# Units 0 and 1 without the first merge, their row steps shared by VectorE and GpSimd; the last row steps of units 2 and 3 on VectorE

## The chip, the cores and the metric

The kernel runs on one core of a Trainium2 chip. The metric is the device time of one execution in microseconds; 2084.89 us is the median of three runs of the kernel before. The engines are named TensorE (PE in the rows, its weight loads PEld), VectorE (DVE), ScalarE (ACT), GpSimd (POOL) and SyncE (SP, which issues most DMAs). Each engine works through a queue of its own, and the queues meet at semaphores.

## The reference, cut to what matters

A delta-rule attention over 768 positions, 4 x 8 heads of size 48, feeds a mixture of 8 experts (all of them computed, mixed by a normalised table P), and then a layer with h cos(h):

```python
def _attn_ref(q, k, v, beta):
    k_n = k / (np.linalg.norm(k, axis=-1, keepdims=True) + 1e-06)
    for t in range(S):
        y[:, :, t] = np.einsum('bhd,bhde->bhe', q[:, :, t], state)
        v_old = np.einsum('bhde,bhd->bhe', state, kt)
        state = state + bt[:, :, :, None] * np.einsum('bhd,bhe->bhde', kt, vt - v_old)
def _moe_ref(x, w_gate, w1, w2):
    ...
    for e in range(E):
        out += P[:, e:e + 1] * (np.maximum(x @ w1[e], 0.0) @ w2[e])
def _moe2_ref(x, w_in, w_out):
    h = x @ w_in
    return (h * np.cos(h)) @ w_out
```

## The kernel before, in words

**Units.** The 768 positions are cut into 12 units of 64 (`C`). Inside a unit the 64 sequential updates of the reference become a triangular system per head: I plus a strictly lower triangular matrix N of beta times the products of keys. Its inverse is made for blocks of 32 (`CB`), for two units at once: 2 units x 16 head pairs (`NS` = 16, four partition groups of 32) lie on the partitions after a 32 x 32 transpose, so that one instruction treats all systems of both units, and a 32 x 32 system lies along the free dimension (`Nsys`, `Xsys`, or `ns0` for units 0 and 1).

**Row steps.** `inv_ops` (line 372) returns a list of 32 closures: the transpose of `Nst` into `Nsys` (VectorE, L374), a select that starts `Xsys` (GpSimd, L377), and the row steps j = 1 to 30. Step j multiplies column j of N, below row j, with row j of the result so far (L388) and adds that to all rows below (L392): two instructions of (31 - j) x j elements per partition, on the engine `eng`, which is GpSimd for all steps. Row j + 1 of the result is complete after step j. The closures are queued in `inv_q`, and `inv_some(n)` takes n of them off and issues them.

**Units 0 and 1** come first. `inv16` (line 399) does row steps on VectorE for both 16 x 16 diagonal blocks at once (14 steps, two instructions each, L408 and L409). The rest is added on TensorE: `merge16_a` multiplies the lower left block of N (`n0`, masked with `m16`), `merge16_y` (VectorE) scales with beta, `merge16_b` multiplies with the first block's inverse, and `merge16_c` adds the result to `tx` and transposes it into `dm`. `tx` and `dm` hold the inverse in its two orientations.

**From the inverse on.** For unit u: `pe_Z1` and `pe_Z2` (TensorE, evictions by ScalarE into `W` and by VectorE into `Bs`) extend the inverse from 32 to 64, `pe_KS` subtracts what the state already gives (`D`), `pe_U` multiplies with the inverse and VectorE writes `U` (L532), `pe_S` adds to the state `S`, `pe_PU` and `pe_QS` make the output rows `Y`, and `pe_XT` transposes them into `xb`, the expert layer's input. The first expert matmul (`H`, L139) needs `xb` of units 0 and 1. In the dense part `half()` issues expert matmuls in between (`moe0_h`, `moe0_y`, evicted by `relu_split`, L156 and L157).

**What sets the order.** Everything is issued under a manual schedule: each engine's queue holds its instructions in the order in which the Python code calls them. The prologue (from `warm(48, p23)` on) is written out by hand; behind it, `tick(u, seq)` walks through the strings in `SEQ`, a letter per step ("U" is `pe_U`, "r" empties `inv_q` and makes `dm`, "R" makes `tx`, "i" starts the next system, "m" is an expert half step, a digit picks the unit). `beta_raw`, `go_beta`, `raw`, `norm_*` and `n_dve` in the prologue scale with beta and the norms; `pp_mask` and `pp_ev` apply the causal mask to the query products `Pp`.

Of the kernel before, what the change touches and what calls it, by code (L numbers as in the profile page):

```python
# [38 lines left out]
def kernel(  # L39
# [331 lines left out]

    def inv_ops(nst, nsys, xsys, tmp, eng):

        ops = [lambda: nc.vector.transpose(out=nsys, in_=nst.rearrange("p s t -> p t s"))]  # L374
# [21 lines left out]
        return ops


    def inv16(xsys, tmp):
        def blk(t0, i0, dt, di, n, j):  # L400
            a = xsys[:, t0:t0 + 1, i0:i0 + 1]
            return bass.AP(a.tensor, a.offset, [a.ap[0], [16 * CB + 16, 2], [dt, n], [di, j]])

        def step(j):
            n = 15 - j
            a = tmp[:, 0:2 * n * j].rearrange("p (a t i) -> p a t i", a=2, t=n)
            x = blk(j + 1, 0, CB, 1, n, j)
            nc.vector.tensor_tensor(out=a, in0=blk(j + 1, j, CB, 0, n, j), in1=blk(j, 0, 0, 1, n, j), op=ALU.mult)  # L408
            nc.vector.tensor_tensor(out=x, in0=x, in1=a, op=ALU.add)  # L409

        return [lambda j=j: step(j) for j in range(1, 15)]

    def merge16_a(u, n, bank, y=True):
# [8 lines left out]
        if y:
            merge16_y(u, bank)

    def merge16_y(u, bank):
        ym[u] = ap2.tile([128, NS, CB], F32, tag="W", name="ym")
        nc.vector.tensor_tensor(
            out=ym[u][:, :, 0:16], in0=bank[:, 0:NS * 16].rearrange("p (s t) -> p s t", t=16),
            in1=betam[:, u, :, None].to_broadcast([128, NS, 16]), op=ALU.mult,
        )  # L430

    def merge16_b(u, bank, s0=0, s1=NS):
        y = ym[u]
        for s in range(s0, s1):
            for p in range(4):
                r = slice(p * CB, p * CB + CB)
                nc.tensor.matmul(
                    out=bank[r, (NS + s) * 16:(NS + s + 1) * 16], lhsT=dm[r, u * NS + s, :], rhs=y[r, s, 0:16],
                    start=True, stop=True, skip_group_check=True,
                )  # L440
# [257 lines left out]
    with tc.manual_schedule():  # L698
# [171 lines left out]
        for u in range(2):  # L870
            nc.scalar.activation(
                out=betam[:, u].rearrange("p (i m) -> p i m", i=2),
                in_=beta_sb[:, u, 0:NS].rearrange("p (m i) -> p i m", i=2), func=ACTF.Copy, scale=hm[:, 4:5],
            )
# [29 lines left out]
        merge16_b(0, pab[:, 0])
        merge16_b(1, pab[:, 1])
        inv_q.extend(inv_ops(Nst, Nsys, Xsys, tmp, nc.gpsimd))
        inv_some(1)
        merge16_c(0, pab[:, 0])
        bs_act(0)
        inv_some(99)  # L910
        pe_Z1(0, pab[:, 0])
# [1 line left out]
        pe_Z1(1, pab[:, 1])
        pp_ev(1, xs0.rearrange("p a c -> p (a c)").rearrange("p (s c) -> p s c", c=C), p01)
        pe_KS(0)
        nc.vector.transpose(out=beta_x, in_=bw[1].rearrange("p (u t) -> p u t", t=CB))
        pe_Z2(0, p01[:, 0])
        beta_raw_x(0)
# [1012 lines left out]
```

## Time and profile before

| | us |
|---|---|
| median of 3 runs (2082.3 to 2086.13) | 2084.89 |
| the profiled execution, its time | 2088.02 |
| the profiled execution, its span | 2085.9 |
| TensorE busy | 2053.4 |
| VectorE busy | 1461.4 |
| GpSimd busy | 905.7 |
| ScalarE busy | 866.1 |

All rows below come from one profiled execution, in microseconds from the start of its span. A busy share is an average over the whole span; which engine ends last in a stretch is read from the windows and the waits of that stretch.

### The profile page before, as it was taken

The numbers are of one execution on the slowest core, as the hardware profiler recorded it, in microseconds if no ns is written. First come the engines' busy times: TensorE is split into PE (matmuls) and PEld (weight loads), VectorE is DVE, ScalarE is ACT, GpSimd is POOL, SyncE is SP. The second block draws the span as 40 slices with busy tenths as digits, with TensorE's granted clock in tenths as the row PEclk, the third lists the DMA queues.
The fourth block names the chain that finished last, engine by engine and source line by source line (L and its number), as shares of the span: only waits on it lengthen the run. The fifth ranks groups of instructions, "written<-read, shape, count | busy, mean of one in ns | idle before, by whom it ended". The sixth has DMA issues, their size and how long they took to land.

```text
span 2085.9 us, 39694 instructions
## 1 busy us (share of the span) xinstructions
PE 2053.4 (98%) x16132; PEld 1729.9 (83%) x16132; DVE 1461.4 (70%) x2253; ACT 866.1 (42%) x1436; POOL 905.7 (43%) x1012
## 2 busy tenths in 40 slices
PE   7999999999999999999999999999999999999999
PEld 6887888778888888888888888888888889999998
DVE  6665537677677777777767787787788666666665
ACT  3442333344444444434333333333333356666664
POOL 4676660156555655544353333333333343333331
PEclk7899999999999999999999999999999999999999
DMA  5532346765554544453684544535354551011000
GB/s 94 127 94 57 78 127 196 296 237 164 193 172 157 204 169 169 177 179 136 249 302 143 173 151 142 173 120 192 130 174 144 185 201 31 1 31 31 16 16 15
DMA packets 212470, 294.39 MB, mean 141 GB/s; under 512 B 86160, under 2 KB 159344, under 8 KB 212288
## 3 DMA queue, kind: packets, MB, share of 16 engines
q1 hardware_dynamic: 208368, 284.20, 41.3%
q0 software_dynamic: 1664, 6.49, 0.9%
q8 instruction: 126, 2.06, 0.4%
q10 hardware_dynamic: 2256, 1.18, 0.2%
q14 instruction: 56, 0.46, 0.1%
HBM read 188.95 MB, written 113.87 MB: 145 GB/s over the span
## 4 chain that ended last, share of the span: by engine, by line
PE 91%; POOL 3%; DVE 2%; SPq 1%; issue 1%; DMA 1%; ACT 1%; ACTq 0%; POOLq 0%; DVEq 0%
PE ps L150 36%; PE ps L1469 27%; PE ps L1759 10%; PE ps L1717 9%; PE ps L139 4%; PE ps L313 1%; POOL w1t L392 1%; POOL w1t L388 1%; PE ps L498 1%; PE ps L281 1%; PE ps L526 1%; PE ps L463 0%; PE ps L556 0%; PE ps L475 0%; PE ps L573 0%
## 5 line engine op out<-in xcount | busy, mean ns | idle before, releaser
L150 PE MATMUL ps<-mh,w2t 128*128 128x512 f32 x3060 | 749.3, 389 | 0.4 <-DVE cth L1505 0.4
L150 PEld LDWEIGHTS ps<-mh,w2t 128*128 128x128 f32 x3060 | 573.5, 188 | 122.0 <-DVE cth L1505 3.3
L1469 PE MATMUL ps<-T,w1t 128*128 128x512 f32 x2520 | 627.2, 389 | 1.9 <-ACT ct L1474 0.8
L1506 POOL TENSOR_TENSOR accp<-accp,cth 128x512 f32<-128x512 f32 x246 | 320.3, 1333 | 562.8 <-DVE cth L1505 562.8
L1469 PEld LDWEIGHTS ps<-T,w1t 128*128 128x128 f32 x2520 | 472.2, 188 | 101.6 <-ACT ct L1474 1.3
L156 ACT ACTIVATE mh<-ps 128x512 fp32r<-128x512 f32 x340 | 203.6, 600 | 620.7 <-PE ps L1469 237.3
L157 DVE SCALAR_TENSOR_TENSOR mh<-ps,mh 128x512 fp32r<-128x512 f32 x340 | 228.8, 688 | 176.8 <-ACT mh L156 175.4
L1474 ACT ACTIVATE scr<-ps 128x512 f32<-128x512 f32 x224 | 134.5, 600 | 163.7 <-PE ps L1469 154.4
L1726 POOL TENSOR_SCALAR tp<-tp 128x512 f32<-128x512 f32 x92 | 91.5, 994 | 204.2 <-ACT tp L1725 204.2
L1505 DVE TENSOR_TENSOR cth<-ps,scr 128x512 f32<-128x512 f32 x246 | 154.3, 684 | 15.2 <-PE ps L150 13.3
L1740 DVE TENSOR_TENSOR tp<-tp,ps 128x512 f32<-128x512 f32 x96 | 66.1, 688 | 133.5 <-ACT tp L1739 133.5
L1477 DVE TENSOR_TENSOR ps<-scr,ps 128x512 f32<-128x512 f32 x168 | 116.5, 694 | 54.6 <-PE ps L1469 53.1
L139 PE MATMUL ps<-xb,w1t 128*128 128x512 f32 (+1 forms) x441 | 111.4, 397 | 0.0
L150 PE MATMUL ps<-h,w2t 128*128 128x512 f32 x396 | 100.8, 400 | 0.0
L1477 DVE TENSOR_TENSOR scr<-ps,scr 128x512 f32<-128x512 f32 x112 | 77.1, 689 | 30.5 <-PE ps L1469 29.2
L139 PEld LDWEIGHTS ps<-xb,w1t 128*128 128x128 f32 x441 | 78.6, 188 | 17.1 <-DVE xb L579 0.9
L1309 DVE TENSOR_TENSOR w1t<-wraw,w1t 128x512 fp32r<-128x512 f32 (+2 forms) x81 | 74.7, 934 | 19.1 <-ACT w1t L1306 17.9
L150 PEld LDWEIGHTS ps<-h,w2t 128*128 128x128 f32 x396 | 73.4, 190 | 15.7 <-issue 0.2
L392 POOL TENSOR_TENSOR w1t<-w1t 128x30 f32<-128x30 f32 (+9 forms) x150 | 80.7, 538 | 11.7
L1717 PE MATMUL ps<-xx,cw 128*128 128x512 f32 x360 | 84.0, 390 | 0.0
L388 POOL TENSOR_TENSOR w1t<-Nsys,w1t 128x30 f32<-128x30 f32 (+9 forms) x150 | 77.9, 520 | 11.4
L1725 ACT ACTIVATE tp<-ps 128x512 f32<-128x512 f32 x96 | 56.2, 586 | 63.5 <-PE ps L1717 63.5
(286 smaller groups left out, 2769.2 us busy)
## 6 DMA issues: line engine op xcount, KB each, us to landing
wss<-w1t SPq DMA_DIRECT2D x56, 768.0 KB
w1t<-wss SPq DMA_DIRECT2D x56, 768.0 KB
w2t<-w2c SPq DMA_DIRECT2D x56, 384.0 KB
T<-tsc SPq DMA_DIRECT2D x22, 512.0 KB
scr<-pts SPq DMA_DIRECT2D x44, 256.0 KB
w2c<-in_moe_w_dram SPq DMA_DIRECT2D x28, 384.0 KB
wss<-w1t SPq DMA_DIRECT2D x28, 384.0 KB
w1t<-wss SPq DMA_DIRECT2D x28, 384.0 KB
```

The source lines that it names most:

```text
L139: nc.tensor.matmul(out=ps[:, :nn], lhsT=w[:, a, kk, fs], rhs=x[:, b, kk, c0:c0 + nn], start=(i == 0), stop=(i == 3 * KD - 1),)
L150: nc.tensor.matmul(out=banks[kd], lhsT=w[:, a, f % 2, kd * 128:(kd + 1) * 128], rhs=h[:, b, :], start=(first and b == 0 and a == 0), stop= ...
L156: nc.scalar.activation(out=h[:, 0, :nn], in_=ps[:, :nn], func=ACTF.Relu)
L157: nc.vector.scalar_tensor_tensor(out=h[:, 1, :nn], in0=ps[:, :nn], scalar=0.0, in1=h[:, 0, :nn].bitcast(F32), op0=ALU.max, op1=ALU.subtract,)
L392: eng.tensor_tensor(out=xsys[:, j + 1:, 0:j], in0=xsys[:, j + 1:, 0:j], in1=a, op=ALU.add)
L1469: nc.tensor.matmul(out=bank, lhsT=s_of(n, nm, a), rhs=T[:, b, :], start=start and q == 0, stop=q == 2, skip_group_check=True)
L1474: nc.scalar.activation(out=out, in_=in_, func=ACTF.Copy, scale=scale)
L1477: nc.vector.tensor_tensor(out=out, in0=a, in1=b, op=op)
L1505: nc.vector.tensor_tensor(out=c, in0=yb[kd], in1=pslot[t], op=ALU.mult)
L1506: nc.gpsimd.tensor_tensor(out=a[:, kd, :], in0=a[:, kd, :], in1=c, op=ALU.add)
L1717: nc.tensor.matmul(out=hb2(i), lhsT=net_w1(f, a, kk), rhs=x2[b](c, kk), start=(j == 0), stop=(j == 3 * KD - 1))
L1759: nc.tensor.matmul(out=ybk[t][:, :DM], lhsT=h[:, a, ts], rhs=net_w2(f, c), start=(f == 0 and j == 0), stop=(f == FT2 - 1 and j == 2),)
```

## The change

For units 0 and 1 the first merge goes (`merge16_a`, `merge16_y`, `betam`). `inv16` now runs row steps over all 32 rows for the first 16 columns on VectorE, and the second diagonal block on GpSimd beside it; step 15 is split by rows between the two. The mask `hm[:, 4]` is inverted and applied by ScalarE to a copy of the half-made inverse that takes the place of N in `n0`, and the merge that is left (`merge16_b`) multiplies that with the second block's inverse. Scaling of `Go` for units 0 and 1 and the mask of unit 1 go to GpSimd. `Go` of units 2 and 3 is copied by ScalarE (`raw`) and scaled later on VectorE. Z1, Z2 and U of unit 0, its state and the second beta transpose move into the prologue, in part ahead of the system of units 2 and 3. Of that system's 32 closures the prologue issues all but the last 8, which stand in `inv_last` until the letter "r" of the next tick; `inv_ops` gets `last=22`, from which step on VectorE is used. The later systems stay on GpSimd.

```diff
-SEQ = ("U0 a0 y1 o2 S0 x1 b0 P0 K1 o3 k1 v U1 X0 P1 S1 X1 H0 x2",
+SEQ = ("P0 y1 a0 x1 K1 b0 o2 k1 o3 v U1 X0 P1 S1 X1 H0 x2",
...
-    def inv_ops(nst, nsys, xsys, tmp, eng):
+    def inv_ops(nst, nsys, xsys, tmp, eng, last=CB):
...
         def mul(j):
             n = CB - 1 - j
+            e = nc.vector if j >= last else eng
...
+        def step(eng, t0, i0, j, a, r0=0, r1=CB):
+            r0 = max(r0, t0 + j + 1)
+            n = r1 - r0
+            a = a[:, 0:n * j].rearrange("p (t i) -> p t i", t=n)
+            x = xsys[:, r0:r1, i0:i0 + j]
+            eng.tensor_tensor(
+                out=a, in0=xsys[:, r0:r1, i0 + j:i0 + j + 1].to_broadcast([128, n, j]),
+                in1=xsys[:, t0 + j:t0 + j + 1, i0:i0 + j].to_broadcast([128, n, j]), op=ALU.mult,
+            )
+            eng.tensor_tensor(out=x, in0=x, in1=a, op=ALU.add)
+
+        for j in range(1, 16):
+            step(nc.vector, 0, 0, j, tmp[:, 0:256], 0, CB if j < 15 else 24)
+        for j in range(1, 15):
+            step(nc.gpsimd, 16, 16, j, tmp[:, 256:512])
+        step(nc.gpsimd, 0, 0, 15, tmp[:, 256:512], 24)
...
     def merge16_c(u, bank):
         x = tx[:, u * NS:(u + 1) * NS, 16:32]
-        nc.vector.tensor_tensor(
-            out=x, in0=x, in1=bank[:, NS * 16:2 * NS * 16].rearrange("p (s t) -> p s t", t=16), op=ALU.add
+        nc.vector.scalar_tensor_tensor(
+            out=x, in0=x, scalar=hm[:, 4:5], in1=bank[:, 0:NS * 16].rearrange("p (s t) -> p s t", t=16),
+            op0=ALU.mult, op1=ALU.add,
         )
...
+    def inv16_dm(xsys, n):
+        nc.vector.transpose(
+            out=dm.rearrange("p s j -> p j s")[:, 0:16], in_=xsys.rearrange("p t j -> p j t")[:, 0:16]
+        )
+        for u in range(2):
+            s = slice(u * NS, (u + 1) * NS)
+            nc.scalar.activation(out=n[:, s, 0:16], in_=dm[:, s, 0:16], func=ACTF.Copy, scale=hm[:, 4:5])
...
+        pp_raw(1, xs0.rearrange("p a c -> p (a c)").rearrange("p (s c) -> p s c", c=C), p01)
+        nc.gpsimd.memset(n0[:, :, 16:CB], 0.0)
+        inv16(ns0, W0.rearrange("p s t -> p (s t)"))
+        go_beta(0, nc.gpsimd)
+        go_beta(1, nc.gpsimd)
         v_scale(0, nc.gpsimd)
         pp_mask(0)
-        for x in inv16(ns0, W0.rearrange("p s t -> p (s t)")):
-            x()
-        inv_tx(ns0)
-        inv_dm(ns0)
+        pp_mask(1)
+        inv16_dm(ns0, n0)
+        inv16_tx(ns0, 16)
+        inv16_tx(ns0, 0)
+        merge16_b(0, n0, pab[:, 0])
         norm_red(2)
         norm_red(3)
         norm_a(2, 4)
+        merge16_c(0, pab[:, 0])
+        bs_act(0, 0)
+        merge16_b(1, n0, pab[:, 1])
         norm_b(2, 4)
         norm_sqr(2)
...
+        pe_Z1(0, p01[:, 0])
+        bs_act(0, 1)
         norm_pe(2, pab[:, 0])
+        nc.vector.transpose(out=beta_x, in_=bw[1].rearrange("p (u t) -> p u t", t=CB))
+        beta_raw_x(0)
         beta_raw(2, pab[:, 0])
         n_dve(2, pcd)
         n_dve(3, p23)
...
+        pe_KS(0)
+        pe_Z2(0, p01[:, 1])
         merge16_c(1, pab[:, 1])
...
+        inv_q.extend(inv_ops(Nst, Nsys, Xsys, tmp, nc.gpsimd, 22))
+        inv_some(len(inv_q) - 8)
+        inv_last.extend(inv_q)
+        inv_q.clear()
+        pe_U(0)
+        load_v(2)
+        pe_Z1(1, p01[:, 0])
+        pe_S(0)
+        load_k(5)
...
                 elif c == "r" and u + 1 < NU:
                     inv_some(99)
+                    while inv_last:
+                        inv_last.pop(0)()
                     inv_dm(Xsys)
```

VectorE's queue in the prologue, from the system of units 2 and 3 (`Nsys`) to U of unit 0, before (the bracket names what an instruction waits for):

```order
L374 STREAM_TRANSPOSE Nsys<-w2t 128x1024 [waits Pool_49]
L444 TENSOR_TENSOR tx<-tx,ps_154 128x16x16 [waits PE_49]
L447 STREAM_TRANSPOSE dm<-tx 128x512 [waits DVE_49]
L444 TENSOR_TENSOR tx<-tx,ps_154 128x16x16 [waits PE_49]
L447 STREAM_TRANSPOSE dm<-tx 128x512 [waits DVE_49]
L818 TENSOR_TENSOR scr_192<-ps_154,mask 128x1024
...
L481 SCALAR_TENSOR_TENSOR Bs<-ps_154,hm,Bs 128x16x32 [waits PE_49,Activation_49]
L799 TENSOR_TENSOR beta_x<-beta_x,nrm 128x2x16 [waits DVE_49]
L532 TENSOR_TENSOR U<-ps_154,beta_x 128x2x8x48 [waits DVE_49,PE_49,Activation_49]
```

and after the change, from the two N evictions (`w2t`) on, where `w1t` is the tile that `Xsys` and the scratch of the row steps lie in:

```order
L806 SCALAR_TENSOR_TENSOR w2t<-ps_154,hm,w2t 128x512 x2
L478 SCALAR_TENSOR_TENSOR Bs<-ps_154,hm,Bs 128x16x32 [waits PE_49,Activation_49]
L430 SCALAR_TENSOR_TENSOR tx<-tx,hm,ps_154 128x16x16
L434 STREAM_TRANSPOSE dm<-tx 128x512 [waits DVE_49]
L374 STREAM_TRANSPOSE Nsys<-w2t 128x1024 [waits Pool_49]
L389 TENSOR_TENSOR w1t<-Nsys,w1t 128x198 [waits DVE_49,Pool_49]
L393 TENSOR_TENSOR w1t<-w1t 128x9x22 [waits DVE_49]
L529 TENSOR_TENSOR U<-ps_154,beta_x 128x2x8x48 [waits PE_49]
L543 TENSOR_TENSOR S_185<-S_184,ps_154 128x2x2x192 [waits PE_49]
```

The transpose into `Nsys` has moved behind Bs of unit 0 and the merge of unit 1, and row step 22 (198 elements, then 9 rows of 22) has come between it and U of unit 0.

GpSimd's queue behind the set-up (`ones` is its last instruction), before:

```order
L754 MEMSET ones 128x128
L239 TENSOR_TENSOR v<-v,dv 128x768
L829 TENSOR_TENSOR Pp<-Pp,mask 128x1024
L345 TENSOR_TENSOR w2t<-w2t,beta_sb 128x512 x2
L377 AFFINE_SELECT w1t<-Nsys 128x1024
```

and after, with the row steps of the second block of units 0 and 1 (`scr_192` holds `ns0` and, from `xs0` on, Pp of unit 1, `W_193` the scratch):

```order
L751 MEMSET ones 128x128
L882 MEMSET scr_192 128x32x16
L407 TENSOR_TENSOR W_193<-scr_192 128x14
...
L407 TENSOR_TENSOR W_193<-scr_192 128x120
L411 TENSOR_TENSOR scr_192<-scr_192,W_193 128x8x15
L770 TENSOR_TENSOR Go<-Go,beta_sb 128x512 x2
L239 TENSOR_TENSOR v<-v,dv 128x768
L828 TENSOR_TENSOR Pp<-Pp,mask 128x1024
L828 TENSOR_TENSOR scr_192<-scr_192,mask 128x1024
L345 TENSOR_TENSOR w2t<-w2t,beta_sb 128x512 x2
L377 AFFINE_SELECT w1t<-Nsys 128x1024
```

Thirty row-step instructions, two scalings of Go and a second mask now stand ahead of the beta scaling (L345) of the system of units 2 and 3.

VectorE's queue in the tick that follows, around `dm` of units 2 and 3, before:

```order
L265 TENSOR_TENSOR kr_190<-kr_190,nrm 128x16x48
L157 SCALAR_TENSOR_TENSOR h<-ps_154,h 128x512
L452 STREAM_TRANSPOSE dm<-w1t 128x32x32
L235 TENSOR_REDUCE nrm<-sq 128x16
L248 TENSOR_SCALAR nrm<-nrm 128x16
```

and after:

```order
L265 TENSOR_TENSOR kr_190<-kr_190,nrm 128x16x48
L157 SCALAR_TENSOR_TENSOR h<-ps_154,h 128x512
L389 TENSOR_TENSOR w1t<-Nsys,w1t 128x184
L393 TENSOR_TENSOR w1t<-w1t 128x8x23
L389 TENSOR_TENSOR w1t<-Nsys,w1t 128x168
...
L393 TENSOR_TENSOR w1t<-w1t 128x30
L448 STREAM_TRANSPOSE dm<-w1t 128x32x32
L235 TENSOR_REDUCE nrm<-sq 128x16
```

Steps 23 to 30, sixteen instructions, now stand between h and `dm`.

## Rows read from the trace of the kernel before

**Rows 1.** The page's first part: busy us (share of the span) xinstructions of TensorE.

```profile
PE 2053.4 (98%) x16132; PEld 1729.9 (83%) x16132; DVE 1461.4 (70%) x2253; ACT 866.1 (42%) x1436; POOL 905.7 (43%) x1012
```

**Rows 2.** Windows: length, busy us (x instructions) of PE, PEld, DVE, ACT, POOL, PEclk, DMA.

```profile
25.00:50.00 25.00, 17.66 (x761) 16.29 (x761) 19.11 (x39) 5.51 (x9) 9.49 (x14) 0.50 0.43 91
50.00:75.00 25.00, 21.01 (x675) 19.84 (x676) 12.49 (x16) 6.19 (x10) 22.26 (x36) 0.58 0.54 125
75.00:100.00 25.00, 24.94 (x366) 20.40 (x365) 20.62 (x31) 12.60 (x20) 13.57 (x20) 1.00 0.49 117
```

**Rows 3.** TensorE's waits from 420 us on: total us, times, longest; the first.

```profile
PE ps L1469 <- ACT ct L1474: 0.8, 1, 0.8
```

**Rows 4.** Timeline of PE: start us, us, line, out<-in, xcount [idle before <-releaser].

```profile
43.21 1.90 PE L437 MATMUL ps<-ym,dm 32*32 32x16 f32 x128 [0.55 <-issue]
...
74.48 2.75 PE L139 MATMUL ps<-xb,w1t 128*128 128x256 f32 x18
...
95.56 1.20 PE L463 MATMUL ps<-dm,Go 32*32 32x32 f32 x64
...
97.90 1.06 PE L281 MATMUL ps<-ident,kr 128*128 128x128 f32 x8
```

**Rows 5.** Timeline of DVE, 20 to 57 us, the start's chain.

```profile
24.16 0.27 DVE L408 TENSOR_TENSOR W<-scr 128x112 f32<-128x112 f32 x1
...
27.81 0.19 DVE L409 TENSOR_TENSOR scr<-scr,W 128x28 f32<-128x28 f32 x1
28.03 1.94 DVE L455 STREAM_TRANSPOSE tx<-scr 128x1024 f32<-128x1024 f32 x1
...
31.64 1.78 DVE L235 TENSOR_REDUCE nrm<-sq 128x16 f32<-128x768 f32 x2
...
33.98 0.18 DVE L256 TENSOR_SCALAR nrm<-nrm 128x32 f32<-128x32 f32 x1 [0.30 <-ACT nrm L255]
...
35.65 0.19 DVE L779 TENSOR_TENSOR nrm<-nrm 128x32 f32<-128x32 f32 x1
...
40.85 1.40 DVE L807 SCALAR_TENSOR_TENSOR w2t<-ps,hm,w2t 128x512 f32<-128x512 f32 x2
43.77 1.92 DVE L374 STREAM_TRANSPOSE Nsys<-w2t 128x1024 f32<-128x1024 f32 x1 [1.53 <-POOL w2t L345]
...
46.03 0.71 DVE L447 STREAM_TRANSPOSE dm<-tx 128x512 f32<-128x512 f32 x1
...
56.20 0.96 DVE L532 TENSOR_TENSOR U<-ps,beta_x 128x768 f32<-128x768 f32 x1 [2.30 <-PE ps L526]
```

**Rows 6.** Timeline of POOL, 45 to 76 us: select and row steps of units 2, 3.

```profile
45.76 1.27 POOL L377 TENSOR_SCALAR_AFFINE_SELECT w1t<-Nsys 128x1024 f32<-128x1024 f32 x1 [2.02 <-DVE Nsys L374]
...
47.17 0.25 POOL L388 TENSOR_TENSOR w1t<-Nsys,w1t 128x30 f32<-128x30 f32 x1
47.50 0.26 POOL L392 TENSOR_TENSOR w1t<-w1t 128x30 f32<-128x30 f32 x1
...
57.66 1.18 POOL L388 TENSOR_TENSOR w1t<-Nsys,w1t 128x220 f32<-128x220 f32 x1
...
62.34 1.24 POOL L392 TENSOR_TENSOR w1t<-w1t 128x234 f32<-128x234 f32 x1
...
74.20 0.61 POOL L392 TENSOR_TENSOR w1t<-w1t 128x210 f32<-128x210 f32 x1
```

**Rows 7.** Timeline of DVE, 88 to 120 us, the first tick and beyond.

```profile
89.81 0.68 DVE L157 SCALAR_TENSOR_TENSOR h<-ps,h 128x512 fp32r<-128x512 f32 x1
90.41 2.07 DVE L452 STREAM_TRANSPOSE dm<-w1t 128x1024 f32<-128x1024 f32 x1
...
95.21 2.46 DVE L265 TENSOR_TENSOR kr<-kr,nrm 128x768 f32<-128x768 f32 x1
...
119.25 0.46 DVE L256 TENSOR_SCALAR nrm<-nrm 128x16 f32<-128x16 f32 x1
```

**Rows 8.** Timeline of POOL at 95 us, a weight split.

```profile
95.05 1.82 POOL L129 TENSOR_TENSOR w1t<-stg,w1t 128x768 fp32r<-128x768 f32 x1 [9.48 <-ACT w1t L128]
```

More of the change, by code (lines that the diff above doesn't have):

```diff
@@ L177 @@
     beta_sb = ap1.tile([128, NU, CB], F32, name="beta_sb")
-    betam = ap1.tile([128, 2, NS], F32, name="betam")
+    ap1.tile([128, 2, NS], F32, name="pad2")
     beta_x = ap1.tile([128, NU, CB], F32, name="beta_x")
@@ L391, in mul @@
             )
-            eng.tensor_tensor(out=xsys[:, j + 1:, 0:j], in0=xsys[:, j + 1:, 0:j], in1=a, op=ALU.add)
+            e.tensor_tensor(out=xsys[:, j + 1:, 0:j], in0=xsys[:, j + 1:, 0:j], in1=a, op=ALU.add)
         for j in range(1, CB - 1):
@@ L399, in inv16, with merge16_b @@
     def inv16(xsys, tmp):
[L400 to L413, printed above, removed]
+        def step(eng, t0, i0, j, a, r0=0, r1=CB):
[13 more added lines that the diff above has]
+        step(nc.gpsimd, 0, 0, 15, tmp[:, 256:512], 24)
+    def merge16_b(u, n, bank):
         for s in range(NS):
@@ L421, in merge16_a, with inv16_tx @@
                 )
[L422 to L426, printed above, removed]
-        nc.vector.tensor_tensor(
[L428 to L440, printed above, removed]
     def merge16_c(u, bank):
         x = tx[:, u * NS:(u + 1) * NS, 16:32]
-        nc.vector.tensor_tensor(
-            out=x, in0=x, in1=bank[:, NS * 16:2 * NS * 16].rearrange("p (s t) -> p s t", t=16), op=ALU.add
+        nc.vector.scalar_tensor_tensor(
+            out=x, in0=x, scalar=hm[:, 4:5], in1=bank[:, 0:NS * 16].rearrange("p (s t) -> p s t", t=16),
+            op0=ALU.mult, op1=ALU.add,
         )
         nc.vector.transpose(out=dm[:, u * NS:(u + 1) * NS, :], in_=tx[:, u * NS:(u + 1) * NS, :])
-    ym = {}
+    def inv16_dm(xsys, n):
[5 more added lines that the diff above has]
+            nc.scalar.activation(out=n[:, s, 0:16], in_=dm[:, s, 0:16], func=ACTF.Copy, scale=hm[:, 4:5])
+    def inv16_tx(xsys, t):
+        nc.vector.transpose(out=tx.rearrange("p s t -> p t s")[:, t:t + 16], in_=xsys[:, t:t + 16])
     def inv_dm(xsys):
@@ L479, in pe_Z2 @@
         if u not in Bs:
-            bs_act(u)
+            bs_act(u, 0)
+            bs_act(u, 1)
         nc.vector.scalar_tensor_tensor(
@@ L487, with bs_act @@
     Bs = {}
-    def bs_act(u):
+    def bs_act(u, a):
         x = tx[:, (u % 2) * NS:(u % 2 + 1) * NS, :]
-        Bs[u] = ap2.tile([128, NS, C], F32, tag="Bs", name="Bs", bufs=1)
-        for a in range(2):
-            nc.scalar.activation(out=Bs[u][:, :, a * CB:a * CB + CB], in_=x, func=ACTF.Copy, scale=hm[:, a:a + 1])
+        if a == 0:
+            Bs[u] = ap2.tile([128, NS, C], F32, tag="Bs", name="Bs", bufs=1)
+        nc.scalar.activation(out=Bs[u][:, :, a * CB:a * CB + CB], in_=x, func=ACTF.Copy, scale=hm[:, a:a + 1])
     def state_mms(bank, t, u, keys, more=False):
@@ L739 @@
             )
-            nc.gpsimd.memset(m[0:16, 16:CB], 0.0)
             h_ = hm[r * CB:(r + 1) * CB]
@@ L743 @@
             nc.gpsimd.memset(h_[:, 2 + r % 2:3 + r % 2], -1.0)
-            nc.gpsimd.memset(h_[0:16, 4:5], 1.0)
+            nc.gpsimd.memset(h_[:, 4:5], 1.0)
+            nc.gpsimd.memset(h_[0:16, 4:5], 0.0)
         nc.gpsimd.tensor_copy(out=swap[:, 0:C], in_=ident[:, C:128])
@@ L756 @@
         inv_q = []
+        inv_last = []
         def inv_some(n):
@@ L869 @@
         n_act(2, pcd)
[L870 to L874, printed above, removed]
+        raw(2, pcd)
         norm_sq(2, "D")
@@ L903 @@
         n_dve(3, p23)
[L904 to L911, printed above, removed]
-        merge16_c(1, pab[:, 1])
[L913 to L918, printed above, removed]
+        pe_KS(0)
+        pe_Z2(0, p01[:, 1])
+        merge16_c(1, pab[:, 1])
+        inv_q.extend(inv_ops(Nst, Nsys, Xsys, tmp, nc.gpsimd, 22))
[7 more added lines that the diff above has]
+        load_k(5)
         nc.scalar.activation(out=wg[:, :, 0, :], in_=wg_sb, func=ACTF.Copy)
@@ L996, in tick @@
                 elif c == "o":
-                    gk_o(u, (pcd, p23)[u % 2])
+                    go_beta(u, nc.vector)
                 elif c == "x":
```

7 lines of the change are left out of this document (2 added, 5 removed).

## The prediction

> **What bounds the kernel now.** I read the busy shares first, then the first 100 us in windows, then TensorE's waits, and last the timelines of VectorE, GpSimd and TensorE around the places that the change touches. TensorE is busy for 2053.4 of 2085.9 us, so it idles 32.5 us in all [rows 1]. The windows show where: 25 to 50 leaves 7.3 us idle, 50 to 75 leaves 4.0, 75 to 100 leaves 0.1, and the granted clock is 0.50 and 0.58 before 75 (its 1.2 GHz level nearly all the time) and 1.00 behind (2.4 GHz) [rows 2]. After 420 us no single wait is over 0.8 us [rows 3]. So the program has two parts: a start that is a chain of dependences between engines, up to the first expert matmul at 74.48 [rows 4], and then a dense part that TensorE fills. Nothing in the dense part could give time back to a late start: whatever moves the first expert matmul, or opens a hole behind it, moves the end by as much.
>
> The chain of the start runs: VectorE's row steps for units 0 and 1, the merges on TensorE, the norms of units 2 and 3, their system in `Nsys` at 43.77, U of unit 0 written by VectorE at 56.20 [rows 5], then state, second unit, X, first expert matmul. GpSimd's 60 row-step instructions for units 2 and 3 start at 47.17 [rows 6] and lie beside all that; nobody in the start waits for the last of them.
>
> **The change, part by part.**
> *Row steps of units 0 and 1.* Before, 28 VectorE instructions of 28 to 112 elements. Those at 24.16 (112 elements, 0.27 us) and 27.81 (28 elements, 0.19) give about 1 ns per element; from the one to the other 13 instructions with 1092 elements take 3.65 us, which leaves 0.19 us each beside the elements [rows 5]. Now VectorE has 30 instructions with 4720 elements: 30 x 0.19 + 4720 x 0.00104 = 10.6 us, from 20.3 to 30.9 where it was done at 28.0. GpSimd has 30 instructions at the same time, 28 of 14 to 56 elements and two of 120. Its nearest row is 128x30 at 0.25 us, 0.33 from start to start [rows 6]; the 28 cost about 9.7 us and the pair about 1.0, so 31.1 if nobody disturbs it. The last pair needs VectorE's step 14, and VectorE's next transpose needs that pair.
> What two engines on this do to each other is not shown at this size. Bounds: nothing (31), or strict turns of whole instructions (20.4 + 10.6 + 10.7 = 41.7). The nearest row is the 16-element instruction at 119.25, which took 0.46 beside GpSimd's steps [rows 7] where its like take 0.17 to 0.18 [rows 5]. GpSimd's operands there are four times as long as here, so I take 2 us for the whole: **done at 33**, with 31 to 41 kept as ends.
> A large pair shows the same thing: VectorE's 768-element scaling at 95.21 took 2.46 us where GpSimd's subtraction ran from 95.05 to 96.87, so it got through only after that [rows 7, 8].
> The Trainium skill, "SBUF — State Buffer", section on the shared ports, has a rule against this part of the change: a VectorE instruction with two SBUF inputs and a GpSimd instruction that reads SBUF exclude each other, the later one blocking for the whole of the other. The large pair agrees; the small one, with 0.29 us lost, agrees less clearly. By the rule the steps would be done near the upper end, which is rival 2 below.
>
> *From there to GpSimd's row steps for units 2 and 3.* Three half transposes (half of 1.94 each) to 36; the masked copy on ScalarE and the one merge that is left (128 TensorE records in 1.90 us [rows 4]) run beside the last of them and are done at about 37 to 38.5. Two reductions 1.8 to 37.8 and the clamp to 38.0, merge add (256 elements, half of an N eviction's 0.70) and transpose 0.4 + 0.7 to 39.3. The norm chain took from 33.98 to 35.84 before: 1.9, to 41.2. The moved beta transpose and scaling 0.75, to 42. TensorE's two norm matmuls must wait for the chain and for Z1 of unit 0: 0.9, to 42.9. Small copies 0.3, two N evictions 1.40, to 44.6; Bs of unit 0 as long as one eviction, 0.7 (its Z2 ends 44.9), to 45.7; merge of unit 1 1.1, to 46.8; transpose into `Nsys` 1.92, to 48.7; select 1.27, to 50.0 [rows 5, 6]. So the steps start at **50.1**, 2.9 later than at 47.17. What fell away (the first merge, its VectorE multiplications, VectorE's share of Go, one mask) is smaller than what VectorE got ahead of `Nsys`: the longer steps, the beta transpose and Bs of unit 0. GpSimd's new masks and Go, about 8 us from 33, are done by 41 to 42, before the N evictions come.
>
> *The step that stands alone.* `inv_ops` now gives steps j >= 22 to VectorE; these are j = 22 to 30, nine of them. The prologue holds back the last **eight** entries. Step 22 is therefore issued at once: its two instructions (198 elements) stand in VectorE's queue right behind the transpose into `Nsys` and **ahead of U of unit 0** (the order shows the wait for GpSimd there). Step 22 needs row 22 of the result, which GpSimd completes in step 21. VectorE takes its queue in order, so U, and behind it the state, Bs of unit 1, the weight split, D and all that TensorE needs next, stand until GpSimd has done 21 steps. Before, 47.17 to 74.81 (the end of the last 128x210), of which three instructions of 1.18 to 1.24 us where their neighbours take 0.6 beside VectorE's wide subtractions; VectorE will be silent now, so 27.64 - 1.8 = **25.9 us** [rows 6]. 50.1 + 25.9 = 76.0; step 22 itself 0.8; U starts at **76.8 instead of 56.20: 20.6 us late**. TensorE has U's matmuls and Z1 of unit 1 done by 50 and then nothing until U is written.
>
> *From U to the first expert matmul.* 18.3 us before (56.20 to 74.48). Z2 of unit 1 now comes behind U's release (up to 1.9 more); the wide VectorE work has no GpSimd beside it and TensorE fewer stops (up to 2 less). I put it at **0**, with 2.5 either way.
>
> *The eight held back.* 16 VectorE instructions, 1824 elements: 16 x 0.19 + 1824 x 0.00104 = 4.9 us, put between the h at 89.81 and the `dm` transpose at 90.41 [rows 7]. VectorE hardly idles there. TensorE's Z1 of unit 2 came at 95.56, 3.1 us behind the transpose's end at 92.5, so it now waits 1.8; the transposes of unit 5's k at 97.90 came 0.2 behind the scaling that ends at 97.67 [rows 4, 7], so they take the rest: **4.7 us**. In return GpSimd is rid of nine steps, for which nobody waited.
>
> *Cost nothing:* the two Go copies of units 2 and 3 on ScalarE, for whose next result VectorE waits only at the merge, unit 1's mask on GpSimd, the loads of v and k moved ahead (issue times only; their buffers come free as late as U and the state do), the set-up of `hm`.
>
> **Sum.** 20.6 + 0 + 4.7 = 25.3 us. On the profiled execution 2085.9 becomes 2111.2 of span; that execution took 2088.0, 3.1 above the median of 2084.89, so on the median scale 2110.2. I predict **2110**.
>
> **The rivals.**
> 1. *The change as its words have it (faster).* If step 22 does not hold VectorE up, because the wait that counts is on an early GpSimd instruction, U starts when its matmuls are done: Bs at 45.7, matmuls 2.2, so about 48 instead of 56.20, 8.2 us gained; less 4.7 for the eight steps, 3.5 gained: 2081. It decides from 21 GpSimd steps taking under some 6 us. Against it: 25.9 us of rows, and row 22 is written by each of these steps. Chance 0.04.
> 2. *The two engines take turns on the row steps.* Done at 38 to 41.7 instead of 33, everything behind it 5 to 8.7 later: about 2117. For it: the pair at 95. Against it: elements of 14 to 56 hold little. Chance 0.15.
> 3. *VectorE catches up.* With TensorE held for long, weights split and beta work done, VectorE may have the slack for the eight steps, and GpSimd, idle, no longer lengthens VectorE's instructions: 2 to 4 us less, about 2106. Chance 0.2.
> 4. *The clock.* TensorE idles 26 us ahead of U; if the 2.4 GHz level, which came 4 us ahead of the first expert matmul before, comes some 8 us later, the dense work until then takes half as long again or twice as long: 3 to 5 us, about 2114. Chance 0.13.
> 5. *Same:* the delay is taken up later. 0.8 us at most in a later wait [rows 3] say no. Chance 0.02.
>
> **How the numbers follow.** The forecast itself has 0.46. Its own bounds are 31 instead of 33 (-2), +-2.5 behind U, and 2 instead of 4.7 for the eight steps. Low end: 2110 - 2 - 2.5 - 2.7 is 2102.8; with rival 3 I take 2102. High end: 2110 + 2.5 + 5 or more of rival 2, 2118. Faster by over 0.2% is rival 1, 0.04; within 0.2% (4.2 us, about what a measurement can tell here) 0.02; slower 0.94.
>
> **What would show it.** On VectorE: the row steps of units 0 and 1 end near 33; idle time of about 26 us ahead of the 198-element instruction, released by GpSimd; U at about 77. On TensorE: about 25 us of waiting for U, first expert matmul near 95, then a stop of 2 to 3 us each at Z1 of unit 2 and at the transposes behind it. On GpSimd: 42 row-step instructions from about 50 to 76 without doubled durations. The prediction is wrong if the 198-element instruction runs before GpSimd's 128x10x21 step, or if the first expert matmul comes before 85.

## The result, and the profile of the changed kernel

| us | before | after | predicted |
|---|---|---|---|
| median (4 runs each) | 2083.60 | 2112.89 (2110.34 to 2114.15) | 2110 (2102 to 2118) |
| ratio to before, 95% interval | 1 | 1.0140 (1.0122 to 1.0157) | 1.012 |
| profiled execution, span | 2085.9 | 2111.4 | 2111.2 |
| GpSimd's row steps of units 2, 3 start | 47.17 | 50.64 | 50.1 |
| U of unit 0 | 56.20 | 76.98 | 76.8 |
| first expert matmul | 74.48 | 93.03 | 95 |
| Z1 of unit 2 | 95.56 | 116.00 | |
| transposes of unit 5's k | 97.90 | 121.14 | |
| Z2 of unit 2 | 100.95 | 126.67 | |

The change makes the kernel 1.4% slower, 29.3 us by the medians and 25.5 us by the two profiled executions. The page's busy line answers [rows 1]: TensorE works 5 us less than before in a span 25.5 us longer.

```profile
PE 2048.4 (97%) x15876; PEld 1724.7 (82%) x15876; DVE 1465.8 (69%) x2269; ACT 866.2 (41%) x1439; POOL 906.4 (43%) x1028
```

Windows of after, columns as in [rows 2]. From 50 to 75 almost only GpSimd works: TensorE 0.44 us, ScalarE 0.71, VectorE nothing.

```profile
25.00:50.00 25.00, 18.03 (x644) 16.72 (x645) 22.01 (x43) 7.48 (x12) 17.11 (x27) 0.50 0.48 102
50.00:75.00 25.00, 0.44 (x18) 0.30 (x12) 0.00 (x0) 0.71 (x2) 21.86 (x42) 0.50 0.11 20
75.00:100.00 25.00, 18.44 (x627) 16.30 (x628) 16.16 (x22) 9.56 (x14) 1.14 (x2) 0.86 0.45 109
100.00:125.00 25.00, 20.61 (x266) 17.08 (x265) 20.50 (x44) 8.27 (x13) 5.17 (x3) 0.89 0.45 114
```

Timeline of VectorE, the places that [rows 5, 7] show of before: the row steps of units 0 and 1, two small instructions of the norm chain, the transpose into `Nsys`, step 22 and U, then the eight held-back steps, `dm` and a scaling of k.

```profile
21.14 0.17 DVE L407 TENSOR_TENSOR W<-scr 128x30 f32<-128x30 f32 x1
...
31.88 0.36 DVE L411 TENSOR_TENSOR scr<-scr,W 128x120 f32<-128x120 f32 x1
32.63 1.08 DVE L437 STREAM_TRANSPOSE dm<-scr 128x512 f32<-128x512 f32 x1 [0.38 <-POOL scr L411]
...
37.14 1.26 DVE L248 TENSOR_SCALAR nrm<-nrm 128x32 f32<-128x32 f32 x1
...
39.69 1.01 DVE L256 TENSOR_SCALAR nrm<-nrm 128x32 f32<-128x32 f32 x1
...
47.26 1.89 DVE L374 STREAM_TRANSPOSE Nsys<-w2t 128x1024 f32<-128x1024 f32 x1
76.30 0.37 DVE L389 TENSOR_TENSOR w1t<-Nsys,w1t 128x198 f32<-128x198 f32 x1 [27.15 <-POOL w1t L393]
76.70 0.37 DVE L393 TENSOR_TENSOR w1t<-w1t 128x198 f32<-128x198 f32 x1
76.98 0.95 DVE L529 TENSOR_TENSOR U<-ps,beta_x 128x768 f32<-128x768 f32 x1
...
108.95 0.34 DVE L389 TENSOR_TENSOR w1t<-Nsys,w1t 128x184 f32<-128x184 f32 x1
...
113.94 1.92 DVE L448 STREAM_TRANSPOSE dm<-w1t 128x1024 f32<-128x1024 f32 x1
...
118.59 2.45 DVE L265 TENSOR_TENSOR kr<-kr,nrm 128x768 f32<-128x768 f32 x1
```

The row at 76.30 carries the result: VectorE stands 27.15 us for GpSimd, and U is the next instruction behind it. Timeline of GpSimd, answering [rows 6]: its row steps of units 0 and 1, the two masks, and its steps of units 2 and 3, the last of which (step 21) ends at 76.26, the moment VectorE goes on.

```profile
31.23 0.37 POOL L411 TENSOR_TENSOR scr<-scr,W 128x14 f32<-128x14 f32 x1
...
36.02 2.34 POOL L828 TENSOR_TENSOR Pp<-Pp,mask 128x1024 f32<-128x1024 f32 x1
38.32 2.35 POOL L828 TENSOR_TENSOR scr<-scr,mask 128x1024 f32<-128x1024 f32 x1
...
50.64 0.25 POOL L389 TENSOR_TENSOR w1t<-Nsys,w1t 128x30 f32<-128x30 f32 x1
...
75.68 0.58 POOL L393 TENSOR_TENSOR w1t<-w1t 128x210 f32<-128x210 f32 x1
```

The two small instructions of VectorE at 37.14 and 39.69 end, at 38.40 and 40.70, as the two masks on GpSimd end (38.36 and 40.67). Before, the like of the second took 0.18 us [rows 5], and that of the first, in the timeline of VectorE before:

```profile
33.46 0.23 DVE L248 TENSOR_SCALAR nrm<-nrm 128x32 f32<-128x32 f32 x1
```

Timeline of TensorE, answering [rows 4]. The first row is what the stall of VectorE does to it; the rows from 116.00 on carry three short stops ("issue" means that the engine waited for nothing that the profile shows).

```profile
77.99 1.53 PE L538 MATMUL ps<-U,kr 64*48 64x48 f32 x64 [27.55 <-DVE U L529]
...
93.03 2.76 PE L139 MATMUL ps<-xb,w1t 128*128 128x256 f32 x18
...
116.00 1.20 PE L459 MATMUL ps<-dm,Go 32*32 32x32 f32 x64 [1.83 <-DVE dm L448]
...
119.38 0.36 PE L313 MATMUL ps<-KT 48*64 48x64 f32 x7 [1.17 <-issue]
121.14 1.94 PE L281 MATMUL ps<-ident,kr 128*128 128x128 f32 x8 [1.40 <-DVE kr L265]
122.73 4.01 PE L139 MATMUL ps<-xb,w1t 128*128 128x512 f32 x9
126.67 1.20 PE L471 MATMUL ps<-tx,W 32*32 32x32 f32 x64
```

Windows of after, same columns, around the two places where the clock changes (PEclk, the granted clock, is the third number from the end): it rises at 82 and falls between 119 and 121, where the mean of 0.64 puts the fall at about 119.6.

```profile
80.00:82.00 2.00, 2.00 (x80) 1.91 (x75) 0.57 (x1) 0.70 (x1) 0.00 (x0) 0.50 0.40 77
82.00:84.00 2.00, 1.89 (x110) 1.73 (x108) 0.64 (x1) 2.00 (x5) 0.00 (x0) 0.99 0.22 40
...
119.00:121.00 2.00, 0.36 (x7) 0.20 (x6) 2.00 (x2) 1.24 (x3) 2.00 (x2) 0.64 0.00 0
121.00:123.00 2.00, 1.86 (x9) 1.89 (x10) 2.00 (x3) 0.00 (x0) 1.72 (x1) 0.50 0.67 205
123.00:125.00 2.00, 2.00 (x6) 1.53 (x5) 1.66 (x3) 1.03 (x1) 0.86 (x1) 0.50 0.57 166
125.00:127.00 2.00, 2.00 (x25) 1.32 (x25) 0.00 (x0) 0.16 (x1) 0.20 (x1) 0.65 0.83 179
```

### The profile page after: what moved, and what is told of

It reads as the page before. It is cut to its first block, busy times and chain, and to the rows that moved or that the text cites. A ratio compares the mean times of both kernels' runs of the same rounds, so it can differ in the third digit from the quotient of the medians.

```text
span 2111.4 us, 39221 instructions
## 1 busy us (share of the span) xinstructions
PE 2048.4 (97%) x15876; PEld 1724.7 (82%) x15876; DVE 1465.8 (69%) x2269; ACT 866.2 (41%) x1439; POOL 906.4 (43%) x1028
## 4 chain that ended last, share of the span: by engine, by line
PE 90%; DVE 4%; POOL 3%; issue 1%; SPq 1%; DMA 1%; ACT 1%; ACTq 0%; POOLq 0%; DVEq 0%
PE ps L150 36%; PE ps L1473 27%; PE ps L1763 9%; PE ps L1721 9%; PE ps L139 3%; POOL w1t L393 1%; POOL w1t L389 1%; PE ps L313 1%; PE ps L495 1%; PE ps L281 1%; PE ps L471 1%; PE ps L553 0%; PE ps L459 0%; PE ps L538 0%; PE ps L523 0%
## 5 line engine op out<-in xcount | busy, mean ns | idle before, releaser
L1730 POOL TENSOR_SCALAR tp<-tp 128x512 f32<-128x512 f32 x92 | 91.2, 992 | 204.2 <-ACT tp L1729 204.2
L393 POOL TENSOR_TENSOR w1t<-w1t 128x30 f32<-128x30 f32 (+9 forms) x141 | 74.6, 529 | 11.0
L1282 POOL TENSOR_TENSOR w2t<-w2t 128x768 fp32r<-128x768 f32 x28 | 55.2, 1972 | 55.2 <-ACT w2t L1278 55.2
```

Of the source, the lines that this page charges most:

```text
L393: e.tensor_tensor(out=xsys[:, j + 1:, 0:j], in0=xsys[:, j + 1:, 0:j], in1=a, op=ALU.add)
```

## The experiments

Ten kernels were run beside the kernel before. Ratios are to it on the same chip, with 95% intervals; places are from one profiled execution of each kernel. The theory: step 22's two instructions, issued at once, hold VectorE's queue ahead of U until GpSimd has done 21 steps; the eight held-back steps cost about 5 us more at Z1 of unit 2 and the transposes.

| kernel | ratio | U of unit 0 | first expert matmul | Z1 of unit 2 | Z2 of unit 2 | expert matmul to Z2 |
|---|---|---|---|---|---|---|
| before | 1 | 56.20 | 74.48 | 95.56 | 100.95 | 26.5 |
| after | 1.0140 | 76.98 | 93.03 | 116.00 | 126.67 | 33.6 |
| e1_hold9 | 1.0021 (1.0009 to 1.0033) | 49.67 | 69.60 | 93.50 | 104.36 | 34.8 |
| e2_last23 | 1.0013 (1.0001 to 1.0024) | 49.04 | 68.41 | 91.50 | 101.19 | 32.8 |
| e3_all_gpsimd | 1.0013 (1.0003 to 1.0022) | 48.99 | 68.66 | 92.31 | 102.90 | 34.2 |
| e4_before_step22 | 1.0145 (1.0127 to 1.0162) | 82.10 | 97.60 | 120.57 | 131.14 | 33.5 |
| e7_last12 | 1.0108 (1.0091 to 1.0125) | 71.76 | 88.86 | 111.84 | 122.43 | 33.6 |
| e6_no_eight | 1.0103 (1.0088 to 1.0119) | 77.06 | 96.25 | 117.80 | 123.10 | 26.9 |
| e5_before_hold9 | 1.0033 (1.0023 to 1.0044) | 53.53 | 71.05 | 94.83 | 104.52 | 33.5 |
| e8_last26_k5 | 1.0008 (0.9999 to 1.0017) | 49.05 | 66.75 | 91.08 | 100.98 | 34.2 |
| e9_last26_m | 1.0040 (1.0027 to 1.0054) | 49.13 | 67.46 | 100.38 | 106.21 | 38.8 |
| e10_last23_m | 1.0034 (1.0020 to 1.0047) | 49.06 | 68.39 | 101.25 | 106.78 | 38.4 |

**Is it step 22?** Three kernels take it out of VectorE's way in three manners: hold nine entries back, let VectorE begin at step 23, or leave all steps to GpSimd.

```diff
 e1_hold9 (against after)
-        inv_some(len(inv_q) - 8)
+        inv_some(len(inv_q) - 9)
 e2_last23 (against after)
-        inv_q.extend(inv_ops(Nst, Nsys, Xsys, tmp, nc.gpsimd, 22))
+        inv_q.extend(inv_ops(Nst, Nsys, Xsys, tmp, nc.gpsimd, 23))
 e3_all_gpsimd (against after)
-        inv_q.extend(inv_ops(Nst, Nsys, Xsys, tmp, nc.gpsimd, 22))
-        inv_some(len(inv_q) - 8)
+        inv_q.extend(inv_ops(Nst, Nsys, Xsys, tmp, nc.gpsimd))
+        inv_some(len(inv_q))
```

> The changed kernel with one number changed: the prologue holds back nine closures instead of eight, so that row step 22 goes to the later tick with the others. Theory (step 22 ahead of U holds VectorE's queue for 27 us): U of unit 0 is written at about 49 instead of 76.98, the first expert matmul comes at 65 to 68 instead of 93.0, nine steps then cost TensorE 5 to 8 us in the tick; time 2081 to 2085, about 29 us under the changed kernel. Rival (the row steps on two engines and the longer prologue are what costs, the queue only shows it): the first expert matmul stays behind 85 and the time above 2100.

> The changed kernel with row steps on VectorE from 23 on instead of 22, eight held back: what its words say. GpSimd does step 22 beside U. Theory: as with nine held back, U at about 49, first expert matmul at 65 to 68, one step (0.8 us) less on VectorE in the tick; time 2080 to 2084. Rival: above 2100.

> The changed kernel with all 30 row steps of units 2 and 3 on GpSimd, all issued in the prologue, none held back. Theory: U at about 49, first expert matmul at 65 to 68; GpSimd's steps run from 50.6 for 38 us to about 89, so the transposes into dm wait until then and VectorE stands meanwhile; TensorE loses there what the start gained, and the time is 2081 to 2086, like the kernel before. If the eight steps on VectorE were the larger part of the loss, it would be under 2078; if the start were slow by itself, above 2100.

The stall is gone in all three, U comes at 49.0 to 49.7, and they run at 1.0013 to 1.0021, about 1.2% under after. So step 22 alone costs 1.2%, some 25 us, and what else is new in the prologue brings U 6.5 to 7.2 us earlier than the 56.20 of [rows 5]. They came later than expected all the same: first expert matmul at 68.4 to 69.6 where 65 to 68 was expected, and 2091.0, 2089.2 and 2089.9 us against at most 2085, 2084 and 2086. That the early start is worth nothing in the end is taken up below.

**Does it work in the old prologue, and does the stall follow the count of steps?** e4 gives the kernel before the same `last=22` and eight held-back closures, nothing else; e7 lets VectorE begin at step 12.

```diff
 e4_before_step22 (against before: only inv_ops with last, hold-back and inv_last)
+        inv_q.extend(inv_ops(Nst, Nsys, Xsys, tmp, nc.gpsimd, 22))
+        inv_some(len(inv_q) - 8)
 e7_last12 (against after)
-        inv_q.extend(inv_ops(Nst, Nsys, Xsys, tmp, nc.gpsimd, 22))
+        inv_q.extend(inv_ops(Nst, Nsys, Xsys, tmp, nc.gpsimd, 12))
```

> The kernel before with only the split of the system of units 2 and 3 taken from the change: steps from 22 on go to VectorE, eight closures held back, units 0 and 1 and the order of the prologue as before. Theory: step 22 stands in VectorE's queue behind the merge of unit 0 and ahead of that of unit 1; VectorE waits from about 47 until GpSimd's step 21 (47 + 26 = 73), so everything behind comes 24 to 27 us later, and the eight steps add 5 to 7: 2110 to 2118. Rival (the longer prologue of the change is the loss): 2088 to 2092.

> The changed kernel with row steps on VectorE from 12 on instead of 22, still eight held back: steps 12 to 22 now stand ahead of U. Theory: VectorE waits only until GpSimd's step 11 (62.3), then does eleven steps in 9.4 us (22 x 0.19 + 5016 x 0.00104), U at 71.7 instead of 76.98, everything behind 5.3 us earlier: 2106 to 2109. Rival (VectorE waits for something other than GpSimd's steps, so their number does not count): U at 84 or later, 2118 or more.

e4 ran at 2117.73 us and e7 at 2108.79, both within what was expected. Waits of e4 (engine, what, line, releaser: total us, times, longest): the same stall on VectorE, handed on to TensorE through `dm`, which stands behind it in this older order.

```profile
DVE w1t L389 <- POOL w1t L393: 26.1, 1, 26.1
...
PE ps L464 <- DVE dm L448: 26.0, 1, 26.0
```

Waits of e7: with ten steps fewer on GpSimd the stall halves, and VectorE spends part of what it gained on the steps itself; U comes 5.2 us ahead of after's, at 71.76 where 71.7 was expected.

```profile
DVE w1t L389 <- POOL w1t L393: 13.2, 1, 13.2
```

**The eight held back.** e6 leaves them out of after, so that the inverse of units 2 and 3 stays unfinished; e5 has nine of them, without any stall, in the kernel before.

```diff
 e6_no_eight (against after)
-        inv_last.extend(inv_q)
 e5_before_hold9 (against before, with inv_ops and inv_last as in e4)
+        inv_q.extend(inv_ops(Nst, Nsys, Xsys, tmp, nc.gpsimd, 22))
+        inv_some(len(inv_q) - 9)
```

> The changed kernel with the eight steps held back (23 to 30) left out, so the inverse of units 2 and 3 stays unfinished; step 22 stays where it is. Theory: U still at about 77 and the first expert matmul at about 93; the wait at Z1 of unit 2, the wait at the transposes behind it and the drop to 1.2 GHz at 120 to 126 go, 4.7 + 2.4 us: 2104 to 2107. Rival (the eight cost nothing of their own): 2111 to 2114.

> The kernel before with steps 22 to 30 of units 2 and 3 on VectorE and all nine held back to the tick, nothing else of the change. Nothing stands ahead of U of unit 0, so the first expert matmul stays at 74 to 75. What is measured is the block in the tick alone. Theory (VectorE has no idle time there): the block of 18 instructions takes 5.7 us, TensorE waits about 5 us at Z1 of unit 2 and at the transposes behind it, and loses 2 to 3 us more at the 1.2 GHz level behind those waits: 5 to 8 us over the kernel before, 2089 to 2094. Rival (VectorE catches up, since GpSimd no longer lengthens its instructions): 2084 to 2087.

Timeline of TensorE in e6, its Z1 of unit 2, transposes and Z2, all without an idle time in front:

```profile
117.80 1.20 PE L459 MATMUL ps<-dm,Go 32*32 32x32 f32 x64
...
120.03 1.09 PE L281 MATMUL ps<-ident,kr 128*128 128x128 f32 x8
...
123.10 1.20 PE L471 MATMUL ps<-tx,W 32*32 32x32 f32 x64
```

From the first expert matmul to Z2 it takes 26.9 us against 33.6 in after and 26.5 before: the eight steps cost 6.8 us there. The profiled execution of e6 shows less of that in its end, since the granted clock had fallen again ahead of its first expert matmul (0.74, 0.83 and 0.69 in the windows from 86 to 96), which so came at 96.25 instead of 93.03; the median is 4.7 us under after's (2108.23 and 2112.89, on two chips whose kernel before ran at 2087.4 and 2083.6, so by the ratios it is 0.37%, 7.7 us, with some 5 us either way by their intervals). The 2108.23 are 1 us above what was expected. e5 ran at 1.0033, 6.7 us over the kernel before, at the upper end of what was expected; its first expert matmul came at 71.05 where 74 to 75 was expected, and to Z2 it shows 33.5 us for nine steps. By their places both say about 7 us, not 4.7.

**Where the gain of e1 to e3 goes.** Timeline of TensorE in e2:

```profile
68.41 2.87 PE L139 MATMUL ps<-xb,w1t 128*128 128x256 f32 x18
...
91.50 1.20 PE L459 MATMUL ps<-dm,Go 32*32 32x32 f32 x64 [1.82 <-DVE dm L448]
92.63 1.63 PE L313 MATMUL ps<-KT 48*64 48x64 f32 x57
95.07 0.49 PE L313 MATMUL ps<-KT 48*64 48x64 f32 x7 [0.81 <-issue]
96.64 1.94 PE L281 MATMUL ps<-ident,kr 128*128 128x128 f32 x8 [1.08 <-DVE kr L265]
98.23 3.03 PE L139 MATMUL ps<-xb,w1t 128*128 128x512 f32 x9
101.19 1.20 PE L471 MATMUL ps<-tx,W 32*32 32x32 f32 x64
```

The first expert matmul is 6.1 us ahead of [rows 4], Z1 4.1, the transposes 1.3, Z2 0.2 behind. TensorE comes early and meets a `dm` that is hardly early. Timeline of VectorE in e2:

```profile
83.85 0.68 DVE L157 SCALAR_TENSOR_TENSOR h<-ps,h 128x512 fp32r<-128x512 f32 x1
...
89.44 1.91 DVE L448 STREAM_TRANSPOSE dm<-w1t 128x1024 f32<-128x1024 f32 x1
```

The h comes 6.0 us earlier than in [rows 7] (89.81); the eight steps that now stand between it and `dm` take 5.0 of that, and `dm` starts at 89.44 against 90.41. In e3, where no step is on VectorE, it is GpSimd that ends late, having begun its steps at 50.55 instead of 47.17; its waits say so:

```profile
DVE dm L448 <- POOL w1t L393: 5.1, 1, 5.1
```

TensorE stops for 1.82 us at Z1, and the clock falls to its 1.2 GHz level, as in after; in e2 it does so at the end of the window of 91 to 93, ahead of the second and third stop (windows of e2, columns as in [rows 2]):

```profile
91.00:93.00 2.00, 1.50 (x85) 1.49 (x89) 1.65 (x5) 0.59 (x2) 0.00 (x0) 0.98 0.04 8
93.00:95.00 2.00, 1.26 (x49) 1.18 (x42) 1.81 (x6) 2.00 (x4) 1.08 (x1) 0.50 0.00 0
95.00:97.00 2.00, 0.85 (x9) 0.69 (x9) 2.00 (x2) 0.74 (x2) 2.00 (x2) 0.50 0.05 15
```

Three kernels tried to get that gain. e8 splits the last steps more evenly (VectorE from step 26, five held back) and gives one scaling of k to GpSimd; e9 and e10 put an expert half step ahead of Z1 of unit 2, into TensorE's hole, in e8 and in e2.

```diff
 e8_last26_k5 (against after)
-        norm_scale(u, nc.vector)
+        norm_scale(u, nc.gpsimd if u == 5 else nc.vector)
-        inv_q.extend(inv_ops(Nst, Nsys, Xsys, tmp, nc.gpsimd, 22))
-        inv_some(len(inv_q) - 8)
+        inv_q.extend(inv_ops(Nst, Nsys, Xsys, tmp, nc.gpsimd, 26))
+        inv_some(len(inv_q) - 5)
 e9_last26_m (against e8) and e10_last23_m (against e2): the second string of SEQ
-       "m W G E K g m N m e O m r m M t O m w R m Z B t m z B i x m k U W m S P N m X",
+       "m W G E K g m N m e O m r m M t O m w R m m Z B t m z B i x k U W m S P N m X",
```

> A version meant to beat both: the changed kernel with steps on VectorE only from 26 on, all five of these held back to the tick, and the scaling of unit 5's k, which took VectorE 2.46 us beside GpSimd's weight split, on GpSimd ahead of that split. Theory: first expert matmul at 68 to 69 as with 23 as the first step; dm 1 us earlier, the transposes of unit 5's k 2 to 3 us earlier, less or no time at 1.2 GHz behind them: 2 to 5 us under the kernel before. If the waits at Z1 of unit 2 alone drop the clock again: within 2 us of the kernel before.

> The version with VectorE's steps from 26 on and unit 5's k scaled on GpSimd, and in addition one expert half step (9 matmuls of 128x512, 2.2 us) moved in the tick from behind Z2 of unit 2 to ahead of Z1 of unit 2, where TensorE waited 2.9 us for dm. Theory (what the start gained was lost in that wait and in the 1.2 GHz stretch behind it): the wait falls under 1 us, the clock of 75 to 100 rises from 0.81 to 0.95 or more, and the time comes 3 to 6 us under the kernel before. Rival (the later chain through Nsys of units 4 and 5 sets the time, so a filled wait is paid back at about 150): within 2 us of the kernel before.

> The version with row steps on VectorE from 23 on, eight held back, and the same expert half step moved ahead of Z1 of unit 2. Theory: the wait of 1.8 us at Z1 goes, that of 1.1 at the transposes of unit 5's k stays or shrinks, and the stretch at 1.2 GHz (95 to 99) goes: 2 to 5 us under the kernel before. Rival as above: within 2 us of it.

None came out as its theory had it. e8 is level with the kernel before, its second case: `dm` moves only from 89.44 to 89.02, as VectorE now waits 2.7 us for GpSimd's step 25. e9 and e10 are 7.6 and 6.3 us slower than the kernel before, 0.3 and 0.2% slower than without the half step, which neither the theory nor the rival had. Timelines of e10, VectorE and then TensorE, say why:

```profile
89.30 1.91 DVE L448 STREAM_TRANSPOSE dm<-w1t 128x1024 f32<-128x1024 f32 x1
...
96.32 0.68 DVE L157 SCALAR_TENSOR_TENSOR h<-ps,h 128x512 fp32r<-128x512 f32 x1
```

```profile
97.14 4.18 PE L139 MATMUL ps<-xb,w1t 128*128 128x512 f32 x9 [7.61 <-DVE h L157]
101.25 1.41 PE L459 MATMUL ps<-dm,Go 32*32 32x32 f32 x64
```

The half step waits 7.61 us for the eviction of the h before it, which VectorE does at 96.32, behind the steps, `dm`, a norm chain and a scaling. `dm` is there at 91.2, but Z1 now stands behind the half step: 101.25 instead of 91.50, and Z2 at 106.78 instead of 101.19. It is the mechanism of step 22 once more, on TensorE: work put into a hole of an engine holds up what is behind it as long as its own operand comes late. No kernel of the ten beats the kernel before.

## Why the prediction was right, point by point

- **Row steps of units 0 and 1:** 21.14 to 32.63 in after, where this execution reached that point some 0.8 us later than the one of before. VectorE's 30 instructions took 11.1 us (10.6 predicted alone); GpSimd's 11.4 (10.7). So each engine cost the other about 0.7 us, not the 2 that the prediction took. Rival 2, whole turns of the engines, fell: it wanted 38 to 41.7. The rule of the Trainium skill ("SBUF — State Buffer", "SBUF: two separate sides"; a two-input VectorE instruction and a GpSimd one exclude each other for the whole of either) is that rival, and would have ended this part at 41.7, 9 us later; the trace agrees with it for the 768-element scaling at 118.59 (2.45 us, 0.96 for its like at 107.48) and not for these row steps, 30 to 238 elements on VectorE beside 14 to 120 on GpSimd.
- **GpSimd's start:** 50.64 against 50.1, and that close partly by luck. Two 32-element instructions of the norm chain, on VectorE's way to `Nsys`, took 1.26 us (37.14) and 1.01 (39.69) beside GpSimd's masks, where their like took 0.23 and 0.18. These 1.9 us are missing from the prediction, which has nothing for what the masks do to VectorE. Some 1.2 us saved on the row steps and 0.5 on the norm matmuls, which ran beside the moved beta work, made up for most of them. GpSimd's 21 steps took 25.6 us against 25.9: the three instructions of 1.2 us in [rows 6] were indeed neighbours' doing, as the longest is 0.69 here.
- **Step 22 ahead of U:** 76.98 against 76.8, +20.8 us. Shown by e1 to e4 and e7; rival 1 fell with it.
- **From U to the first expert matmul:** 16.05 us against 18.28 before, so -2.2, inside the 2.5 that the prediction allowed around 0. Two more runs have the same queues in this stretch. In e7 the granted clock was 0.50 up to 86 and 0.52 from 86 to 88, and the stretch took 17.10: 1.2 us less than before without help of the clock. TensorE stopped there once, for 0.46 us, where before it stopped for 0.71 and 1.50; this is the prediction's "TensorE fewer stops". The other 1.1 us in after goes with the clock: its matmuls ran at the 2.4 GHz level from 82 on, 11 us ahead of the first expert matmul; before, the clock rose at about 71, 3.5 us ahead. In e6 the clock rose at about 81 and fell again at about 88, and the stretch took 19.19. So rival 4 had the sign wrong for the execution of after and right for that of e6 (0.9 us over before): with the same instructions this stretch differs by 3 us from one execution to another.
- **The eight steps:** 4.99 us on VectorE (4.9 predicted), and TensorE's transposes at +23.24 where the first expert matmul was at +18.55: 4.7, as predicted, though in three stops of 1.83, 1.17 and 1.40 us and not in two of 2 to 3. Rival 3 fell.
- **What the sum lacked:** the clock at that place. Behind the first two of these stops, ahead of the third, the granted clock fell; it was 0.50 from 121 to 125, and nine expert matmuls took 4.01 us where their like at 109.81 take 2.33; Z2 stands at +25.72, another 2.5. So the eight steps cost 7.2, not 4.7; the places of e6 (6.8) and of e5 (7.0, for nine) agree.

20.8 - 2.2 + 4.7 + 2.5 = 25.8, and the span grew by 25.5. The mechanism was right, and step 22 is nearly all of it; the nearness of the prediction's 25.3 is luck, since the -2.2 and the 2.5 that it did not have nearly cancel. The term "the eight held back" was mis-sized by 2.5 us, and "from U to the first expert matmul" by 2.2. All of these are places of one execution on either side. The medians differ by 29.3 us (25.4 to 32.7 by the interval of the ratio), above the 25.3: the profiled execution of before, 2088.02 us, lies 4.4 above the median of its four runs, and no run shows where in it these 4.4 arise.

## What to carry to other kernels

Handing the tail of a serial chain to another engine costs little in instructions and can cost the whole length of the chain in queue order (27 us of waiting here): count the entries held back against the entries that go to the new engine, and read which instructions stand behind the first of them. Before filling a hole of one engine, look at where the filler's own operand stands in its producer's queue. And when a start is made shorter, check the next meeting point of the engines first: here 6 us won at the first expert matmul of e2 were gone at Z2 of unit 2, 33 us later, since the system of units 2 and 3 was ready hardly any earlier.
